# Pairs 0 and 1 of a state-space scan: block-diagonal states and split scaling, and B and C loaded four tokens to a partition

## The chip, the cores and the metric

One core of a Trainium2 chip runs the whole program. The metric is the device time of one execution in microseconds; the runs of a kernel are summed up by their median. All times and durations below are in microseconds (us) unless they are marked ns, and times "at" a point count from the start of the profiled span.

The engines are called as in the profile: PE (matrix multiply; PEld is its weight load, which overlaps), DVE (vector), ACT (scalar), POOL (GpSimd) and SP (which here only issues transfers). DMAs are issued by SP, by ACT and by POOL; those of POOL can also cast from fp32 to bf16.

## The reference

Two parts follow each other. The first is a chunked scan over 768 tokens for 4 batches of 8 heads, with head width 32 (`D`) and state width 16 (`N`):

```python
cum = np.cumsum(np.log(np.clip(a, 1e-06, 1.0))[chunk], axis=-1)
L = np.exp(cum[:, :, :, None] - cum[:, :, None, :]) * causal
M = np.einsum('bhin,bhjn->bhij', Cc, Bc) * L
y = np.einsum('bhij,bhjd->bhid', M, xc)
y += np.einsum('bhin,bhnd->bhid', Cc, state) * np.exp(cum)
state = decay_full * state + sum_j(Bc[j] * xc[j] * decay_from_j)
```

The second is a gated feed-forward network on the 3072 resulting rows of 256: `(relu(y @ w_gate) * (y @ w_val)) @ w_out`, with 1536 hidden units. Inputs and output are fp32; the kernel multiplies in bf16 where it can.

## The kernel before

**Tiles.** Tokens go in chunks of 128, two chunks make a *pair* `p` of 256 tokens of one batch. A batch has 6 chunks (`NC`), so pairs 0, 1 and 2 are batch 0 and pair 3 opens batch 1; there are 12 pairs (`NPAIR`) and 6 blocks `b` of 512 rows (`NBLK`) for the feed-forward part. The cumulative decay is one scan on DVE (`cp`, L210); small fp32 matmuls (`dec_wide`, `dec_token`, `dec_all`, L220 to L247) turn it into scale factors, which are multiplied into C, and their reciprocals into B (or, for pair 0, into x).

**One pair.** B and C are loaded as `bcr` (`load_bc`, L82). For pairs 0 to 3 (`NWIDE`) a partition holds two neighbouring tokens, so that a run of 32 fp32 values (128 B) comes in one piece; for later pairs a run is 64 B. They are scaled into bf16 `bs` (`scale_bc`, L278), transposed on PE (`transp`, L309), and copied out as `BT` (`bevac`) and as two masked versions of `CT` (`cevac`), one for each half of the heads. `G` (L374) multiplies BT and CT for four groups of heads at a time, in row tiles of 32; `gevac` (L388) copies the four banks out as `gs` with the causal mask: ACT copies two of them and POOL clears the upper triangle (`affine_select`), DVE multiplies the other two and half of one by a mask. `back` and `backevac` transpose BT back to token order (`bx`). `astep` (L413) adds B times x into the running state `A_ps` with one 128x128 by 256 matmul; `sevac` (L423) copies it out through the block mask `smask` on DVE as `Sm`, 128x256. `inter` (L484) multiplies `Sm` and CT into y, two matmuls of 128 columns for a chunk; `Dm` (L498) adds `gs` times x, 16 matmuls in column strips of 32. `yevac` (L512) copies y out as bf16 `yT`. `states` and `spread` (L438 and L456) do the states of later pairs in four column strips.

**Feed-forward.** `gvh_mm`, `gvh_relu` and `gvh_mul` do one 128-unit slice `f` of the hidden layer for one pair (256 rows), `gv` (L526) for a block of 512 rows; `fout` (L572) multiplies the hidden block by `wo`.

**Order.** Each engine runs its instructions in the order in which the program writes them (`in_order`, L15), so the order of the text is the schedule. Up to L721 it is written out by hand for pairs 0 and 1: while DVE, ACT and POOL prepare them, PE fills gaps with `keep_warm` matmuls on zeros (L200) and with slices f = 0 to 3 of pair 0. Then the loop over blocks starts (L723). In block 0, pair 1's slices 0 to 3 come first (L744), then slices 4 to 11 of the whole block; pair 2 is turned after slice 5 (L751) and turned back after slice 7, pair 3 is turned between thirds of `fout` (L783).

**Transfers.** SP issues `a`, B of pair 0, one chunk of x of pair 0, B of pair 1; ACT issues C of pair 0, the other chunk of x, C of pair 1. POOL issues the weights in pieces, cast to bf16, and chunk 0 of pair 1's x, also cast (L180). Chunk 1 of that x comes over SP (L656) and is cast by ACT (L692). B and C of pairs 2 and 3 are loaded by SP (`held`, L637, called at L657 and L693); the one-element `memset` in front of each ties its start to DVE's progress. Their scaling on POOL stands at L703 and L721. PSUM has eight banks: five shared ones and one each for the tags `y`, `tp` and `Aps`.

Of the kernel before, what the change touches and what calls it, by code (L numbers as in the profile page):

```python
# [29 lines left out]
def kernel(  # L30
# [39 lines left out]

    NWIDE = 4
    st = {}

    def place(p):
        b, c0 = p // PPB, 2 * (p % PPB)
        return b, c0, slice(c0 * 128, (c0 + 2) * 128)

# [45 lines left out]
    load_bc(0, 0, nc.sync)  # L123
# [9 lines left out]
    def cast_x(p, chunks=(0, 1)):  # L133

        b, c0, sl = place(p)
        if "x" not in st.setdefault(p, {}):
            xb = att.tile([128, 2 * NH * D], BF16, tag="xb", name="xb", bufs=6)
            st[p]["x"] = [xb[:, i * NH * D:(i + 1) * NH * D] for i in range(2)]
        for i in chunks:
# [24 lines left out]
    masks = const.tile([128, 2, 128], BF16)  # L164

    def causal(dst, n, wide):
        pattern = [[0, n], [1, 2], [2, 64]] if wide else [[0, n], [1, 128]]
        if wide:
            dst = dst.rearrange("s k (r m) -> s k r m", r=2)
# [5 lines left out]
    causal(masks[:, 1:2], 1, True)  # L175
    causal(masks[:, 0:1], 1, False)
# [3 lines left out]
    cast_x(1, (0,))  # L180
# [37 lines left out]
    wfac = glob.tile([128, NWIDE, 2, 2, 8], FP32)  # L218
# [54 lines left out]
    def cast_bc(p, eng, js):  # L273
        src, dst = views(p, js)
        for t in range(2):
            copy(eng, dst[:, :, t], src[:, :, t])

    def scale_bc(p, eng, js=slice(0, 2), f=None):  # L278
# [8 lines left out]
        for t in range(2):  # L287
            eng.tensor_tensor(  # L288
                out=dst[:, :, t], in0=src[:, :, t],
                in1=f[:, :, 4 * t:4 * t + 4].to_broadcast([128, n, 4, N]), op=ALU.mult)  # L290

# [41 lines left out]
    def cevac(p, *engs, again=None):  # L333
        s = st[p]
        s["CT"] = CT = att.tile([128, 2, 2, 128], BF16, tag="CT", name="CT")
        src = s["tp"][1].rearrange("s i m -> s (i m)")
        for t in range(2):
# [8 lines left out]
    def ct(p, i, rows=slice(0, 128), t=None):  # L346
        CT = st[p]["CT"]
# [6 lines left out]
    def split(p, ap):  # L354

        return ap.rearrange("s t (r m) -> s t r m", r=2) if p < NWIDE else ap
# [31 lines left out]
    def gevac(p, half=True, early=False, between=None):  # L388
# [3 lines left out]
        wide = p < NWIDE  # L392
        m = masks[:, int(wide):int(wide) + 1].to_broadcast([128, 4, 128])
# [10 lines left out]
        for q in (2, 3):  # L404
            nc.vector.tensor_tensor(out=d[:, q], in0=g[q], in1=m, op=ALU.mult)  # L405
        if half and not early:
# [445 lines left out]
```

## Time and profile before

| what | us |
|---|---|
| median of the 3 runs shown | 128.95 |
| lowest and highest of them | 127.25, 130.51 |
| the profiled execution | 126.84 |
| its span, first to last instruction | 124.8 |
| PE busy in the span | 120.0 |
| DVE, ACT and POOL busy | 92.7, 79.3, 43.3 |

The rows of a timeline give the start, the duration of the group, the engine, the line, the operation with what it writes and reads, the shapes and a count; the bracket says how long the engine stood idle before and what ended that. "Busy" for PE is modelled, because its matmuls overlap. The mean granted clock of PE was 0.999.

### The profile page before, as it was taken

How to read it: one execution, taken by the hardware profiler on the slowest of the kernel's cores; microseconds unless marked ns; L12 is line 12 of the kernel's file. 1: busy time of each engine (PE TensorE's matmuls, PEld its weight loads, DVE VectorE, ACT ScalarE, POOL GpSimd, SP SyncE). 2: the span in 40 equal slices, each digit the busy share in tenths (PEclk: the TensorE clock that was granted, in tenths of full speed). 3: DMA queues.
4: the chain of work that ended last, by engine and by line, in shares of the span. 5: the costliest groups of instructions: out<-in, count | busy, mean ns of one | idle time of the engine just before them, and what ended most of it. 6: DMA issues, size and time to landing. Idle time of an engine off the chain costs nothing.

```text
span 124.8 us, 3396 instructions
## 1 busy us (share of the span) xinstructions
PE 120.0 (96%) x1261; PEld 82.5 (66%) x1268; DVE 92.7 (74%) x223; ACT 79.3 (64%) x177; POOL 43.3 (35%) x80
## 2 busy tenths in 40 slices
PE   5999999999999999999999999999999999999990
PEld 2365664578885477884577875577875677864790
DVE  4678898888889955898865798855888856687510
ACT  4166777734888735787735887645987546886420
POOL 6798939531805062805021703132600033000000
PEclk9999999999999999999999999999999999999999
DMA  2999999995979999389632289912200002200022
GB/s 57 164 160 180 179 203 198 168 135 54 188 69 188 112 108 183 91 86 120 80 55 84 90 79 133 112 24 84 84 5 0 0 0 89 84 0 0 0 89 84
DMA packets 73312, 11.92 MB, mean 95 GB/s; under 512 B 66960, under 2 KB 73296, under 8 KB 73296
## 3 DMA queue, kind: packets, MB, share of 16 engines
q1 hardware_dynamic: 63408, 8.43, 44.4%
q0 software_dynamic: 6336, 2.56, 17.1%
q10 hardware_dynamic: 3552, 0.72, 3.6%
q8 instruction: 10, 0.16, 0.6%
q14 instruction: 6, 0.05, 0.1%
HBM read 11.11 MB, written 3.15 MB: 114 GB/s over the span
## 4 chain that ended last, share of the span: by engine, by line
PE 96%; DVE 1%; issue 1%
PE o L579 25%; PE gv L550 22%; PE val L534 15%; PE gate L531 13%; PE w L203 4%; PE g L382 3%; PE y L505 3%; PE tp L320 2%; PE y L494 2%; PE o L591 1%; PE d L225 1%; PE dall L243 1%; PE A_ps L450 1%; PE A_ps L419 1%; PE bt L363 1%
## 5 line engine op out<-in xcount | busy, mean ns | idle before, releaser
L579 PE MATMUL o<-wo,h 128*128 128x256 bf16 x276 | 33.1, 273 | 0.0
L538 DVE TENSOR_TENSOR h<-r,val 128x512 bf16<-128x512 bf16 x42 | 28.8, 685 | 5.5 <-ACT r L537 3.0
L537 ACT ACTIVATE r<-gate 128x512 bf16<-128x512 f32 x42 | 25.1, 597 | 8.1 <-PE gate L531 7.3
L579 PEld LDWEIGHTS <-h 128*128 128x128 bf16 x276 | 25.9, 98 | 5.4 <-issue 2.1
L560 DVE TENSOR_TENSOR h<-r,gv 128x256 bf16<-128x256 bf16 x60 | 24.8, 421 | 4.3 <-ACT r L557 3.5
L534 PE MATMUL val<-yT,wv 128*128 128x512 bf16 x84 | 25.0, 379 | 0.3
L170 POOL TENSOR_SCALAR_AFFINE_SELECT gs<-gs 128x512 bf16<-128x512 bf16 (+1 forms) x24 | 12.1, 526 | 37.3 <-ACT gs L394 37.3
L557 ACT ACTIVATE r<-gv 128x256 bf16<-128x256 f32 x60 | 22.8, 385 | 3.0 <-PE gv L550 0.8
L531 PE MATMUL gate<-yT,wg 128*128 128x512 bf16 x78 | 23.7, 379 | 0.0
L550 PE MATMUL gv<-yT,wg 128*128 128x256 bf16 x120 | 23.3, 273 | 0.0
L550 PE MATMUL gv<-yT,wv 128*128 128x256 bf16 x120 | 23.0, 273 | 0.0
L405 DVE TENSOR_TENSOR gs<-g,masks 128x512 bf16<-128x512 f32 x24 | 15.4, 684 | 5.0 <-PE g L382 4.5
L288 POOL TENSOR_TENSOR bs<-bcr,fac 128x256 bf16<-128x256 f32 x16 | 9.6, 621 | 16.1 <-DMA bcr<-in_B_dram 12.6
L534 PEld LDWEIGHTS <-wv 128*128 128x128 bf16 x84 | 8.2, 98 | 9.9
L550 PEld LDWEIGHTS <-wv 128*128 128x128 bf16 x120 | 11.7, 98 | 1.9 <-DMA wv<-in_moe_w_val_dram 0.3
L550 PEld LDWEIGHTS <-wg 128*128 128x128 bf16 x120 | 11.2, 98 | 1.9 <-issue 0.2
L394 ACT CAST gs<-g 128x512 bf16<-128x512 f32 x12 | 7.1, 590 | 8.4 <-PE g L382 8.4
L262 ACT CAST yT<-y 128x512 bf16<-128x512 f32 (+1 forms) x14 | 7.1, 527 | 7.7 <-PE y L505 4.1
L531 PEld LDWEIGHTS <-wg 128*128 128x128 bf16 x84 | 7.8, 98 | 6.3
L461 DVE TENSOR_TENSOR Sm<-A_ps,smask 128x256 bf16<-128x256 f32 x15 | 5.8, 418 | 6.3 <-PE A_ps L450 6.3
L608 ACT COPY ob<-o 128x512 f32<-128x512 f32 x10 | 5.9, 585 | 4.7 <-PE o L579 4.7
L344 DVE TENSOR_SCALAR CT<-tp,tmask 128x256 bf16<-128x256 bf16 x23 | 7.0, 343 | 0.3 <-PE tp L629 0.3
(92 smaller groups left out, 106.5 us busy)
## 6 DMA issues: line engine op xcount, KB each, us to landing
xr<-in_x_dram SPq DMA_DIRECT2D x20, 128.0 KB, 3.4
out_dram<-ob SPq DMA_DIRECT2D x10, 256.0 KB, 2.2
bcr<-in_C_dram SPq DMA_DIRECT2D x16, 64.0 KB, 3.1
bcr<-in_B_dram SPq DMA_DIRECT2D x16, 64.0 KB, 3.1
wg<-in_moe_w_gate_dram POOLq DMA_DIRECT2D x3, 256.0 KB, 5.0
wv<-in_moe_w_val_dram POOLq DMA_DIRECT2D x3, 256.0 KB, 6.0
wo<-in_moe_w_out_dram POOLq DMA_DIRECT2D x3, 256.0 KB, 5.2
bcr<-in_B_dram SPq DMA_DIRECT2D x4, 128.0 KB, 6.6
```

The source lines that it names most:

```text
L170: nc.gpsimd.affine_select(out=dst, in_=dst, pattern=pattern, compare_op=ALU.is_ge, fill=0.0, base=0, channel_multiplier=-1)
L262: (eng.copy if eng is nc.scalar else eng.tensor_copy)(out=out, in_=in_)
L288: eng.tensor_tensor(out=dst[:, :, t], in0=src[:, :, t], in1=f[:, :, 4 * t:4 * t + 4].to_broadcast([128, n, 4, N]), op=ALU.mult)
L405: nc.vector.tensor_tensor(out=d[:, q], in0=g[q], in1=m, op=ALU.mult)
L531: nc.tensor.matmul(out=g, lhsT=wg[:, k, fs], rhs=yT[:, k, tk], start=(k == 0), stop=(k == 1))
L534: nc.tensor.matmul(out=v, lhsT=wv[:, k, fs], rhs=yT[:, k, tk], start=(k == 0), stop=(k == 1))
L537: nc.scalar.activation(r, g, AF.Relu)
L538: nc.vector.tensor_tensor(out=fst[b][:, f], in0=r, in1=v, op=ALU.mult)
L550: nc.tensor.matmul(out=gv_[:, j], lhsT=(wg, wv)[j][:, k, fs], rhs=yT[:, k, tk], start=(k == 0 and not (early and j)), stop=(k == 1), skip_ ...
L557: nc.scalar.activation(r[:, 0:256], fst[b, f, u][:, 0], AF.Relu)
L560: nc.vector.tensor_tensor(out=fst[b][:, f, u * 256:(u + 1) * 256], in0=fst.pop((b, f, u, "r"))[:, 0:256], in1=fst.pop((b, f, u))[:, 1], op ...
L579: nc.tensor.matmul(out=o[:, ts % 2], lhsT=fst[b][:, f, ts * 128:(ts + 1) * 128], rhs=wo[:, f], start=(f == 0 and new), stop=(f == NF - 1), ...
```

## The change

It has two halves. *States*: `astep` uses four column strips of 32 and writes only the 64 columns that hold the diagonal blocks; for the states read by pairs 0 and 1 `sevac` is an ACT copy of 128x64, and `inter` multiplies the four 32x32 blocks on their own diagonal tiles of the array (8 matmuls a chunk in place of 2). Later states are spread on DVE as before. Pair 1's B is scaled half on DVE and half on POOL. *Loads*: B of pair 0 comes with four tokens to a partition on 64 partitions, and ACT casts it in two copies; B of pairs 2 and 3 share one tile, 64 partitions each with four tokens to a partition, and so do their C (`load_quad`). They are scaled together on POOL, turned together after slice 8 and turned back together between thirds of `fout`. A run of B or C is then 256 B, and a load has half as many pieces.

Some steps move with it. Both chunks of pair 1's x come over SP, issued behind the first mask product of pair 0, and are cast by POOL and ACT; POOL's cast load of one chunk is gone. Slice 3 of pair 0 and a part of `dec_all` change places around `Dm(1)`. The last two pieces of `wo` are issued ahead of the scaling of pairs 2 and 3, the cast load of pair 2's x behind it. One of four later `keep_warm` matmuls of 512 columns is left out. `cevac` writes its two versions of pair 1 ahead of and behind DVE's share of `yevac(0)`.

The diff, cut to its core (a third mask for four tokens, `R(p)` for the number of tokens to a partition, and the reading of the shared tiles in `ct` are left out):

```diff
+def load_quad(j):
+    if not quad:
+        quad["bcr"] = raw.tile([128, NH, 2, 4, N], FP32, tag="quad", name="bcr4", bufs=1)
+    bcr = quad["bcr"]
+    nc.vector.memset(bcr[:, 0, j, 0, 0:1], 0.0)
+    for p in (2, 3):
+        b, c0, sl = place(p)
+        ps = slice(64 * (p - 2), 64 * (p - 1))
+        nc.sync.dma_start(
+            out=bcr[ps, :, j].rearrange("p h r n -> p h (r n)"),
+            in_=(B, C)[j][b, :, sl, :].rearrange("h (p r) n -> p h (r n)", r=4))
...
-load_bc(0, 0, nc.sync)
+b0r = glob.tile([64, NH, 4, N], FP32)
+nc.sync.dma_start(
+    out=b0r.rearrange("p h r n -> p h (r n)"),
+    in_=B[0, :, 0:256, :].rearrange("h (p r) n -> p h (r n)", r=4))
...
-cast_x(1, (0,))
...
+def dec_quad(dst, p):
+    b, c0, _ = place(p)
+    w, o = c0 // HC, (c0 % HC) * 128
+    ps = slice(64 * (p - 2), 64 * (p - 1))
+    for r in range(4):
+        nc.tensor.matmul(
+            out=dst[ps, r], lhsT=cp[:, o + r:o + 256:4],
+            rhs=pick[:, w, 8 * b:8 * b + 8], start=(r == 0), stop=True,
+            tile_position=(0, 64 * (p - 2)), skip_group_check=True)
...
+def scale_quad(eng):
+    quad["bs"] = bs = att.tile([128, 2, 4, 128], BF16, tag="bs4", name="bs4", bufs=1)
+    for j in (1, 0):
+        for t in range(2):
+            hs = slice(4 * t, 4 * t + 4)
+            eng.tensor_tensor(
+                out=bs[:, j].rearrange("s r (q t n) -> s r t q n", q=4, t=2)[:, :, t],
+                in0=quad["bcr"][:, hs, j].rearrange("s q r n -> s r q n"),
+                in1=qfac[:, j, :, hs].to_broadcast([128, 4, 4, N]), op=ALU.mult)
+def turn_quad():
+    quad["tp"] = tp = mm.tile([128, 2, 4, 128], BF16, tag="tp", name="tp4")
+    for j in range(2):
+        for r in range(4):
+            nc.tensor.transpose(out=tp[:, j, r], in_=quad["bs"][:, j, r], identity=ident)
+    quad["BT"] = att.tile([128, 4, 128], BF16, tag="BT4", name="BT4", bufs=1)
+    quad["CT"] = att.tile([128, 2, 4, 128], BF16, tag="CT4", name="CT4", bufs=1)
+    for p in (2, 3):
+        st.setdefault(p, {})["BT"] = quad["BT"][:, 2 * (p - 2):2 * (p - 1)]
+def bevac_quad(eng):
+    copy(eng, quad["BT"].rearrange("s k (m r) -> s k r m", r=4),
+         quad["tp"][:, 0].rearrange("s r (k m) -> s k r m", k=4))
+def cevac_quad(eng, t):
+    dst = quad["CT"][:, t].rearrange("s r m -> s (r m)")
+    src = quad["tp"][:, 1].rearrange("s r m -> s (r m)")
+    if eng is nc.scalar:
+        eng.mul(dst, src, tmask[:, t:t + 1])
+    else:
+        eng.tensor_scalar_mul(dst, src, tmask[:, t:t + 1])
+def back_quad(eng):
+    bt = mm.tile([128, 4, 128], BF16, tag="tp", name="bt4")
+    for k in range(4):
+        nc.tensor.transpose(out=bt[:, k], in_=quad["BT"][:, k], identity=ident)
+    bx = att.tile([128, 4, 128], BF16, tag="bx4", name="bx4", bufs=1)
+    copy(eng, bx.rearrange("s k m -> s (k m)"), bt.rearrange("s k m -> s (k m)"))
+    for p in (2, 3):
+        st[p]["B"] = [bx[:, 2 * (p - 2) + i] for i in range(2)]
...
+def cevac(p, *engs, again=None, ts=(0, 1)):
...
-def gevac(p, half=True, early=False, between=None):
...
+        if q in after:
+            after[q]()
...
-    nc.tensor.matmul(
-        out=A_ps[0], lhsT=st[p]["B"][i], rhs=st[p]["x"][i],
-        start=(c == 0), stop=(c == NC - 2), skip_group_check=True)
+    xi = st[p]["x"][i].rearrange("s (t q d) -> s q t d", t=2, q=4)
+    for q in range(4):
+        nc.tensor.matmul(
+            out=A_ps[0][32 * q:32 * q + 32, 0, 0:64].rearrange("p (t d) -> p t d", t=2),
+            lhsT=st[p]["B"][i][:, 32 * q:32 * q + 32], rhs=xi[:, q],
+            start=(c == 0), stop=True, tile_position=(0, 32 * q),
+            skip_group_check=True)
...
 def sevac(p, i):
-    if 2 * (p % PPB) + i == NC - 1:
+    c = 2 * p + i + 1
+    if c == NC:
         return
-    S[2 * p + i + 1] = n = att.tile([128, 2, 128], BF16, tag="Sm", name="Sm", bufs=5)
-    nc.vector.tensor_tensor(out=n, in0=A_ps[0], in1=smask, op=ALU.mult)
+    if c < 2 * NTILE:
+        S[c] = n = att.tile([128, 64], BF16, tag="Sd", name="Sd")
+        nc.scalar.copy(out=n, in_=A_ps[0][:, 0, 0:64])
+    else:
+        S[c] = spread_one(0)
...
+def spread_one(k):
+    n = att.tile([128, 2, 128], BF16, tag="Sm", name="Sm", bufs=5)
+    a = A_ps[0][:, 0, 64 * k:64 * k + 64].rearrange("p (t o d) -> p t o d", t=2, o=1)
+    nc.vector.tensor_tensor(
+        out=n.rearrange("p t (q d) -> p t q d", q=4),
+        in0=a.to_broadcast([128, 2, 4, D]),
+        in1=smask.rearrange("p t (q d) -> p t q d", q=4), op=ALU.mult)
+    return n
...
+        if p < NTILE:
+            new = opening(s, t)
+            for q in range(4):
+                r = slice(32 * q, 32 * q + 32)
+                nc.tensor.matmul(
+                    out=s["y"][t][r, i].rearrange("s (r m) -> s r m", r=2),
+                    lhsT=Sm[r, 32 * t:32 * t + 32], rhs=ct(p, i, r, t=t),
+                    start=new, stop=True, tile_position=(32 * q, 32 * q),
+                    skip_group_check=True)
+            continue
...
 new_bs(0)
 dw = bank("dw", (128, 2, 8))
 dec_wide(dw, 0, True)
+b0s = glob.tile([64, 4, 128], BF16)
+for t in range(2):
+    nc.scalar.copy(
+        out=b0s.rearrange("s r (q t n) -> s r t q n", q=4, t=2)[:, :, t],
+        in_=b0r.rearrange("s (t q) r n -> s r t q n", t=2)[:, :, t])
+tpb = bank("tpb", (128, 4, 64), BF16)
+for r in range(4):
+    nc.tensor.transpose(out=tpb[:, r], in_=b0s[:, r], identity=ident[0:64, 0:64])
+st[0]["BT"] = att.tile([128, 2, 128], BF16, tag="BT", name="BT")
+copy(nc.scalar, st[0]["BT"].rearrange("s k (m r) -> s k r m", r=4),
+     tpb.rearrange("s r (k m) -> s k r m", k=2))
 d01 = mm.tile([128, 2, 2, 8], FP32, tag="Aps", name="d01")
 dec_token(d01[:, 0], 0, True)
-cast_bc(0, nc.scalar, B_)
 scale_bc(0, nc.vector, C_, dw)
 r0 = const.tile([128, 2, 8], FP32)
 nc.vector.reciprocal(r0, d01[:, 0])
 to_x(0, nc.gpsimd, r0.rearrange("s i h -> s (i h)"))
-transp(0, 0, True)
-bevac(0, nc.scalar)
 transp(0, 1, True)
...
-gevac(0, between=lambda: backevac(0, nc.scalar))
-new_x(1)
-nc.vector.memset(st[1]["xr"][0:1, 1, 0, 0:1], 0.0)
-load_x(1, 1, nc.sync)
-held(2, with_x=False)
-keep_warm(3)
-d23 = mm.tile([128, 2, 2, 8], FP32, tag="tp", name="d23")
-dec_wide(d23[:, 0], 2, True)
+def load_x1():
+    new_x(1)
+    nc.vector.memset(st[1]["xr"][0:1, :, 0, 0:1], 0.0)
+    for i in range(2):
+        load_x(1, i, nc.sync)
+gevac(0, between=lambda: backevac(0, nc.scalar), after={2: load_x1})
+load_quad(1)
+keep_warm(2)
+d23 = mm.tile([128, 4, 8], FP32, tag="tp", name="d23")
+dec_quad(d23, 2)
 astep(0, 0)
-dec_wide(d23[:, 1], 3, False)
-nc.scalar.copy(out=wfac[:, 2:4, 1], in_=d23)
+sevac(0, 0)
+dec_quad(d23, 3)
+nc.scalar.copy(out=qfac[:, 1], in_=d23)
 keep_warm(1)
-sevac(0, 0)
 scale_bc(1, nc.vector, C_)
-scale_bc(1, nc.gpsimd, B_)
+scale_bc(1, nc.vector, B_, ts=(1,))
+scale_bc(1, nc.gpsimd, B_, ts=(0,))
 weights(4, 8)
+new_xb(1)
+def x1(eng, i):
+    copy(eng, st[1]["x"][i], st[1]["xr"][:, i].rearrange("s h d -> s (h d)"))
+x1(nc.gpsimd, 0)
 Dm(0, True)
 inter(0, 1)
+transp(1, 1, True)
 astep(0, 1)
-transp(1, 1, True)
 transp(1, 0, True)
+cevac(1, nc.vector, ts=(0,))
 yevac(0, nc.scalar, nc.vector)
 bevac(1, nc.scalar)
-cevac(1, nc.vector)
+cevac(1, nc.vector, nc.vector, ts=(1,))
 sevac(0, 1)
...
 back(1)
 gevac(1, early=True, between=lambda: backevac(1, nc.scalar))
-copy(nc.scalar, st[1]["x"][1], st[1]["xr"][:, 1].rearrange("s h d -> s (h d)"))
-held(3, with_x=False)
+x1(nc.scalar, 1)
+load_quad(0)
 weights(8, NF)
 weights_out(0, 4)
-for f in (1, 2, 3):
+for f in (1, 2):
     gvh_mm(0, f, 0)
     gvh_relu(0, f, 0)
+dall = mm.tile([128, HC, 2, NB, 8], FP32, tag="tp", name="dall")
+dec_all(dall, range(2))
 astep(1, 0)
 sevac(1, 0)
-nc.vector.reciprocal(wfac[:, 2:4, 0], wfac[:, 2:4, 1])
-new_bs(2)
-scale_bc(2, nc.gpsimd)
+nc.vector.reciprocal(qfac[:, 0], qfac[:, 1])
 weights_out(4, 8)
 weights_out(8, NF)
+scale_quad(nc.gpsimd)
+cast_x(2)
 Dm(1, "shared")
 inter(1, 0)
 inter(1, 1)
 astep(1, 1)
 yevac(1, nc.scalar, nc.vector)
-dall = mm.tile([128, HC, 2, NB, 8], FP32, tag="tp", name="dall")
-dec_all(dall, range(HC))
+gvh_mm(0, 3, 0)
+gvh_relu(0, 3, 0)
+dec_all(dall, range(2, HC))
 for f in range(4):
     gvh_mul(0, f, 0)
 for w in range(2):
     nc.scalar.copy(
         out=fac[:, :, w * HC:(w + 1) * HC, 1, :].rearrange("p b k h -> p k b h"),
         in_=dall[:, :, w])
-new_bs(3)
-cast_x(2)
-scale_bc(3, nc.gpsimd)
...
         if b == 0:
-            if f == 5:
-                turn(P)
-                tevac(P, nc.scalar, nc.vector)
-            if f == 7:
-                back(P)
-                backevac(P, nc.vector)
+            if f == 8:
+                turn_quad()
...
+            if f == 10:
+                cevac_quad(nc.scalar, 1)
...
             if third == 1:
-                turn(Q)
-                tevac(Q, nc.scalar, nc.vector)
+                back_quad(nc.scalar)
...
-        back(Q)
-        backevac(Q, nc.vector)
```

## The prediction

> **What bounds the kernel now.** I read the page first (shares, then the 40 slices), then the chain of waits over the opening, then the timeline of each engine from 5 to 16 us, then the DMA issues one at a time.
>
> ```profile
> PE 120.0 (96%) x1261; PEld 82.5 (66%) x1268; DVE 92.7 (74%) x223; ACT 79.3 (64%) x177; POOL 43.3 (35%) x80
> ...
> PEclk9999999999999999999999999999999999999999
> DMA  2999999995979999389632289912200002200022
> ```
>
> PE's 96% is two different things. From 15.5 us on the chain is PE behind PE, a 512-column pair each 0.43 us, and nothing else ends last. Before that PE is busy on paper (4.02 us are warming matmuls) while the end is set by a relay between engines. So a gain or loss is either an earlier or later start of the dense stretch, or PE work or PE waits inside it. The relay:
>
> ```profile
> 5.34 0.50 ACT L262 CAST bs<-bcr 128x128 bf16<-128x128 f32 x2 [3.04 <-DMA bcr<-in_B_dram]
> ...
> 6.22 0.29 PE L320 MATMUL tp<-ident,bs 128*128 128x128 bf16 x2
> ...
> 7.16 0.40 PE L382 MATMUL g<-CT,BT 32*128 32x256 bf16 x8
> ...
> 7.67 1.05 POOL L299 TENSOR_TENSOR xb<-xr,r 128x512 bf16<-128x512 f32 x1 [0.29 <-DMA xr<-in_x_dram]
> ...
> 7.68 1.29 DVE L405 TENSOR_TENSOR gs<-g,masks 128x512 bf16<-128x512 f32 x2 [0.20 <-PE g L382]
> ...
> 8.68 1.03 POOL L170 TENSOR_SCALAR_AFFINE_SELECT gs<-gs 128x512 bf16<-128x512 bf16 x2
> ...
> 9.76 0.41 PE L505 MATMUL y<-gs,xb 128*32 128x128 bf16 x16
> ...
> 10.78 0.59 DVE L344 TENSOR_SCALAR CT<-tp,tmask 128x256 bf16<-128x256 bf16 x2
> ...
> 11.50 0.40 PE L382 MATMUL g<-CT,BT 32*128 32x256 bf16 x8
> ...
> 13.75 0.41 PE L505 MATMUL y<-gs,xb 128*32 128x128 bf16 x16
> ```
>
> Pair 0's B lands at 5.34; G(0) runs at 7.16; from 7.68 to 11.37 DVE hardly rests; POOL, late because x of pair 0 lands only at 7.6, releases Dm(0) at 9.76; DVE's C copies release G(1) at 11.50. In the dense stretch one other arrival is near the edge:
>
> ```profile
> 17.76 1.19 POOL L288 TENSOR_TENSOR bs<-bcr,wfac 128x256 bf16<-128x256 f32 x2 [1.99 <-DMA bcr<-in_B_dram]
> ...
> 22.43 1.19 POOL L288 TENSOR_TENSOR bs<-bcr,wfac 128x256 bf16<-128x256 f32 x2 [0.22 <-DMA bcr<-in_B_dram]
> ```
>
> These are B of pairs 2 and 3, issued at 10.39 and 14.04: 7.2 and 8.2 us on the way, because the weights share the DMA engines (205 GB/s from 13.7 to 21.5 us, of which SP's own 393 KB are about 50).
>
> What a packet costs, from three stretches with one kind of load (64 B runs, 128 B runs, 1 KB output rows; the last columns are clock, DMA share and GB/s):
>
> ```profile
> 41.00:43.00 2.00, 2.00 (x14) 0.98 (x12) 1.85 (x5) 1.62 (x4) 0.00 (x0) 1.00 0.93 95
> ...
> 43.00:44.50 1.50, 1.50 (x14) 1.05 (x13) 1.17 (x3) 0.79 (x2) 0.64 (x2) 1.00 1.02 152
> ...
> 49.00:49.50 0.50, 0.50 (x12) 0.38 (x5) 0.50 (x2) 0.50 (x2) 0.00 (x0) 1.00 1.11 343
> ```
>
> 95, 152 and 343 GB/s over 16 engines are 10.8, 13.5 and 48 ns a packet; a line through them puts 256 B at about 18 to 19 ns.
>
> **The change, part by part.**
>
> *B of pair 0 as 512 packets of 256 B.* Behind `a` the SP queue shares each DMA engine with ACT's queue: 64 packets of 13.5 ns beside 64 others is 1.7 us, which with `a` through at 2.9 (153 GB/s flow from 2 to 3 us) and 0.7 us to its signal (seen at 3.6) gives the 5.34 seen. 32 of 19 beside 32 of 13.5 are 1.0 us: B lands near 4.65. Ends: 5.34 (bytes alone count), 4.65; I take 4.7. ACT then casts two 64x256 blocks, 0.43 each by the 128x256 cast of x (0.50 for both before, now about 0.8): done by 5.5. Four transposes (0.22 issued) replace two (0.11), but PE is held until 5.54 by dw in any case; `dec_token` now stands behind them (0.32) and ends at 6.1, before C's scaled block (6.16). So the C transposes stay at 6.22, G(0) at 7.16: 0. Without the early landing: casts to 6.15, transposes and `dec_token` to 6.7, G(0) 0.5 late. x of pair 0, behind B on SP and no longer joined by the POOL cast of pair 1, comes at 7.0 to 7.5.
>
> *POOL and DVE to G(1).* POOL loses a DMA issue (0.90) and half of pair 1's B scaling (0.42); with x at 7.2 its selects end near 9.3 instead of 9.71. DVE loses the 0.41 spread at 9.23 but gains memsets (0.06 each) and B's half (0.35 by the neighbouring 128x128 row), and its yT copy now stands behind the first C copy (0.34). Sum: 9.24 + 0.06 + 0.69 + 0.35 + 0.34 + 0.45 + 0.34 less overlaps of 0.1: C done near 11.3 (11.37 before). Dm(0) comes 0.3 earlier, G(1) 0.1 earlier: DVE takes the rest of the gain back. wv (landed at 11.06) is awaited inside this as before.
>
> *x of pair 1 on SP.* Two loads issued at 8.4 (behind the first mask) replace one at 9.35 and one POOL cast. The old one landed at 12.85: less 1.3 us until data flows (as for `a`, 0.80 to 2.1) and 0.7 to the signal, 1.5 of transfer. Two from 9.75 are then done at 9.75 + 3.0 + 0.7 = 13.4, or at 12.2 by the 152 GB/s of an empty queue. ACT wants it at 13.0. Between: 0.15 late, and behind it on ACT stand two relus, the new state copy and y. I charge +0.15.
>
> *States as diagonal blocks.* Three 0.41 spreads leave DVE, three 128x64 copies come to ACT at about 0.21 (the 128x32 copy took 0.18, the 128x96 one 0.24). The last spread, 13.86 to 14.28, had held inter(1,1); the copy ends near 14.1: -0.15. Each state step is four 64-column matmuls on four column strips (12 such issue in 0.10 to 0.18) for one of 0.11: -0.05 each, all but one in the opening's slack. inter has 8 small matmuls for 2; no row has its shape. Ends: 0.11, four at once as for the 16 of L505, or 0.44, one after another. I take 0.11, since its blocks share neither rows nor strips.
>
> The weight loader stands 0.21 us idle before each row-tiled G and before the 128-wide load behind it, but at 52.46 a 128-wide matmul follows column strips with no gap. So three new changes (one around inter(1,.), two around state(2,0), which stood between `fout` matmuls) cost 0 to 0.6; I take a third, +0.2. The Trainium skill (TensorEngine Tiling (Array Packing), Key Properties) says that every change of the tiling mode drains TensorE; by that rule all three cost 0.21 and the sum below would be 0.4 higher.
>
> *f = 3, dall.* Before, six dall matmuls (0.81) behind y(1) and DVE's first product (15.42) both held gvh(0,0,1) to 15.47. Now 0.44 of f = 3 and 0.27 of dall stand there, and 0.54 of dall stands ahead of Dm(1), where PE waits for masks. DVE's product decides: y 0.1 earlier, so -0.1. `keep_warm` (3 to 2) takes 0.21 from a stretch where PE waits for POOL: 0.
>
> *Quads.* 12 transposes before, 12 after. ACT's copies grow (0.58 and 0.69 at f = 8 and 10 for 0.37 at f = 5; it has 0.27 spare per 0.87 us step), DVE's shrink (0.61 for 0.60 and 0.60). Covered by PSUM banks and PE's own 0.45 of transposes; `bx4` (ACT, near 27.9) is just in time for the state step at 28.0: 0 to +0.2, taken as 0. POOL's four 0.60 scalings are the same four, but all must end before the turn at 21.5 (17.2 + five steps of 0.87): B of both pairs must land by 20.3, where pair 3's had until about 25. SP's queue: x to about 12.5, then 262 KB of C and 262 KB of B. At 128 B, SP got 50 GB/s, 41 ns a packet and engine: 13.5 its own, 27.5 waiting. 256 B: 46.5 ns if only its own part grows, 88 GB/s, B at 19.2; if all grows like its own part (1.42 times), 71 GB/s, B at 20.6; with no gain 50 GB/s, B at 23.7. I take 19.2, since the packet was mostly waiting: no wait.
>
> Sum: -0.1 (G(1)), +0.15 (x), -0.15 (state copy), -0.1 (f = 3), +0.2 (mode changes): 0.0. The profiled run took 126.84 us, its span 124.8 and 2.0 around it; the median of the runs shown is 128.95 (127.25 to 130.51). Forecast: no change, 126.8 on the profiled run's scale, 129.0 on the median's.
>
> **Rivals.**
> 1. *PE waits at the turn for B of pairs 2 and 3* (the other side). For: one deadline for two pairs, two more POOL weight loads pulled ahead of it, today's 8.2 us. Against: half the packets. Price: landing + 1.25 (two scalings) - 21.5; 0.35 at 71 GB/s, 3.4 at 50, so 129.3 to 132.4. It decides from a landing after 20.3, and passes 2% after 22.9.
> 2. *B of pair 0 doesn't land earlier.* G(0) 0.5 late, DVE passes all of it on: 129.5.
> 3. *Diagonal blocks run one by one.* inter(0,1) hides behind DVE, the two of pair 1 do not: +0.66, less 0.1 of slack: 129.6. No row speaks for it. The Trainium skill (TensorEngine Tiling (Array Packing), Gotcha 1: PSUM Pressure) says that different row tiles can't use one PSUM bank at the same time, and all four blocks write one bank; no run here shows it so far.
> 4. *Landings bring more.* x of pair 0 at 6.9 and pair 1's at 12.2, C scaled in 0.5 as at 5.68: -0.15, -0.2, -0.3: 128.3.
>
> **How the numbers follow.** Forecast 0.46 (128.5 to 129.5), rival 1 0.25, rival 2 0.08, rival 3 0.07, rival 4 0.14. About 2% (2.6 us) is what a measurement of this kernel can tell from no change. Only rival 1's far half passes it: 0.12, and 0.06 for the scatter of runs on top of rivals 1 to 3: slower 0.18. No case gains 2.6; rival 4 with the scatter (1.3% to either side of the median) gives faster 0.08; same 0.74. The range takes in rival 4 and the runs' scatter below (127.6) and rival 1 to a landing at 22.4 us above (131.2).
>
> **What would show it.** B's cast at 4.7 and G(0) at 7.2; Dm(0) near 9.4, G(1) near 11.4; inter's 8 matmuls issued in 0.11 to 0.15; gvh(0,0,1) at 15.3 to 15.6; transposes of the quad straight behind the val matmuls of f = 8, the scaling on POOL ended before. Wrong if PE stands before the turn, if G(0) slips, or if the dense stretch starts after 16.

## The result, and the profile after

The changed kernel takes 133.98 us (median of 4 runs, 133.29 to 134.19) against 129.73 for the kernel before on the same chip (4 runs, 127.25 to 130.65): 1.045 times, 95% interval 1.0313 to 1.0586. The forecast was 129.0. The runs of the kernel before lie near 127 or near 130.5, with a few between; ratios here leave the longer, disturbed runs out, medians take in all. The profiled execution of the changed kernel took 133.29, its span 131.4 (before 126.84 and 124.8).

The posts of the relay that the prediction read, as starts in us from each span's beginning:

| | before | forecast | after |
|---|---|---|---|
| cast of B of pair 0 (ACT) | 5.34 | 4.7 | 6.14 |
| G(0) | 7.16 | 7.2 | 8.80 |
| Dm(0) | 9.76 | 9.4 | 13.47 |
| G(1) | 11.50 | 11.4 | 16.05 |
| Dm(1) | 13.75 | none given | 18.87 |
| gvh(0,0,1), the dense stretch begins | 15.47 | 15.3 to 15.6 | 20.63 |
| end of the span | 124.8 | 124.8 | 131.4 |

Of 6.6 us, 5.2 are lost before the dense stretch and 1.4 in it (109.3 to 110.8). The timeline of the changed kernel's opening (start, duration, engine, line, operation, and in brackets the idle time before it with its releaser):

```profile
6.14 0.71 ACT L722 CAST b0s<-b0r 64x256 bf16<-64x256 f32 x2 [3.84 <-DMA b0r<-in_B_dram]
...
6.90 0.29 PE L727 MATMUL tpb<-ident,b0s 64*128 64x64 bf16 x4 [1.52 <-ACT b0s L722]
...
7.23 0.73 ACT L295 COPY BT<-tpb 128x256 bf16<-128x256 bf16 x1 [0.38 <-PE tpb L727]
...
8.60 0.17 ACT L743 COPY wfac<-d 128x16 f32<-128x16 f32 x1 [0.29 <-PE d L258]
...
8.80 0.61 PE L457 MATMUL g<-CT,BT 32*128 32x256 bf16 x8
...
10.52 1.03 PEld L248 LDWEIGHTS d<-pick,cp 64*64 64x64 f32 x8 [0.84 <-issue]
...
13.47 0.62 PE L608 MATMUL y<-gs,xb 128*32 128x128 bf16 x16
...
14.02 0.40 PE L588 MATMUL y<-CT,Sd 32*32 32x128 bf16 x8
```

B arrives 0.8 later, not 0.6 sooner. PE takes its instructions in order, so it stands 1.52 us in front of the transposes of `b0s`, with `dec_token` and C's transposes queued behind. G(0) is 1.64 late: 0.80 from the arrival, 0.21 from a longer cast, some 0.3 on ACT from a copy of BT that takes 0.73 for 0.37, and some 0.3 in which ACT then waits for the decay matmuls queued behind `b0s` (row 8.60, whose result G(0) needs). The eight decay loads of one pair, 1.03 at 10.52, had taken a third of that in the kernel before:

```profile
8.35 0.33 PEld L225 LDWEIGHTS d<-pick,cp 64*64 64x64 f32 x8 [0.42 <-issue]
```

From G(0) to G(1) the rows of PE that kept their shape are a third to a half longer than before (G(0) 0.61 for 0.40, Dm(0) 0.62 for 0.41, two transposes 0.39 for 0.28). The clock says why. First the page's slices, then four stretches of the same trace (length; busy us and instructions of PE, PEld, DVE, ACT, POOL; granted clock; DMA share; GB/s):

```profile
PEclk9965579999999999999999999999999999999998
```

```profile
6.00:7.00 1.00, 0.10 (x4) 0.10 (x4) 0.00 (x0) 0.71 (x2) 0.36 (x1) 1.00 1.62 129
...
7.50:8.00 0.50, 0.50 (x8) 0.30 (x7) 0.26 (x1) 0.50 (x2) 0.01 (x1) 0.55 1.53 170
8.00:12.00 4.00, 4.00 (x37) 2.45 (x37) 3.05 (x10) 1.75 (x6) 2.93 (x5) 0.50 0.90 145
...
18.00:20.00 2.00, 2.00 (x50) 1.40 (x49) 0.91 (x4) 1.30 (x5) 2.00 (x5) 1.00 0.18 8
```

PE was busy 0.10 of the microsecond from 6 to 7; at 7.6 its granted clock is halved, stays at 0.50 for ten microseconds and is back at 1.00 at 17.8. In the dense stretch the turn of the quad and G(2):

```profile
25.62 1.19 POOL L325 TENSOR_TENSOR bs<-bcr,qfac 128x256 bf16<-128x256 f32 x2 [2.38 <-DMA bcr<-in_B_dram]
...
26.27 0.59 PE L637 MATMUL val<-yT,wv 128*128 128x512 bf16 x2
...
26.86 0.45 PEld L334 LDWEIGHTS <-bs 128*128 128x128 bf16 x8 [0.49 <-POOL bs L325]
26.87 0.62 PE L334 MATMUL tp<-ident,bs 128*128 128x128 bf16 x8
...
27.52 1.30 ACT L295 COPY BT<-tp 128x512 bf16<-128x512 bf16 x1 [0.45 <-PE tp L334]
...
30.98 0.28 PE L457 MATMUL g<-CT,BT 32*128 32x256 bf16 x3
...
31.57 0.37 PE L457 MATMUL g<-CT,BT 32*128 32x256 bf16 x5 [0.30 <-DVE bcr L752]
```

B of pairs 2 and 3 comes last. The 0.49 is idle time of the weight loader; PE itself loses about 0.17, since a pair of 512 columns takes 0.43 from start to start and the turn starts 0.60 behind the last `val`. The copy of BT takes 1.30 us where 0.58 was forecast; G(2) is then split by a wait (its eight matmuls start at 30.98 and 31.57).

### The profile page after: what moved, and what is told of

The parts are those of the page before. It is cut to its first block, busy times and chain, and to the rows that moved or that the text cites. A ratio compares the mean times of both kernels' runs of the same rounds, so it can differ in the third digit from the quotient of the medians.

```text
span 131.4 us, 3466 instructions
## 1 busy us (share of the span) xinstructions
PE 124.7 (95%) x1302; PEld 85.0 (65%) x1302; DVE 90.8 (69%) x216; ACT 82.9 (63%) x181; POOL 42.8 (33%) x80
## 4 chain that ended last, share of the span: by engine, by line
PE 73%; ACT 1%; issue 0%; DVE 0%
PE o L682 23%; PE gv L653 17%; PE val L637 11%; PE gate L634 11%; PE y L608 3%; PE g L457 3%; PE y L597 1%; PE tp L389 1%; PE o L694 1%; ACT yT L295 1%; PE A_ps L548 1%; DVE ob L697 0%; PE bt L355 0%; PE A_ps L500 0%
## 5 line engine op out<-in xcount | busy, mean ns | idle before, releaser
L634 PE MATMUL gate<-yT,wg 128*128 128x512 bf16 x84 | 25.0, 379 | 0.0
L653 PE MATMUL gv<-yT,wg 128*128 128x256 bf16 x120 | 23.9, 278 | 0.3 <-ACT yT L295 0.3
L653 PE MATMUL gv<-yT,wv 128*128 128x256 bf16 x120 | 23.6, 277 | 0.0
L295 ACT CAST yT<-y 128x512 bf16<-128x512 f32 (+1 forms) x14 | 8.2, 624 | 8.2 <-PE y L608 4.1
L653 PEld LDWEIGHTS <-wg 128*128 128x128 bf16 x120 | 11.4, 100 | 2.0 <-issue 0.2
L525 DVE TENSOR_TENSOR Sm<-A_ps,smask 128x256 bf16<-128x256 f32 x17 | 6.6, 419 | 7.1 <-PE A_ps L548 6.5
L415 DVE TENSOR_SCALAR CT<-tp,tmask 128x256 bf16<-128x256 bf16 x19 | 5.9, 344 | 2.9 <-PE tp L389 2.7
```

Source lines behind the costliest of these rows:

```text
L295: (eng.copy if eng is nc.scalar else eng.tensor_copy)(out=out, in_=in_)
L634: nc.tensor.matmul(out=g, lhsT=wg[:, k, fs], rhs=yT[:, k, tk], start=(k == 0), stop=(k == 1))
L653: nc.tensor.matmul(out=gv_[:, j], lhsT=(wg, wv)[j][:, k, fs], rhs=yT[:, k, tk], start=(k == 0 and not (early and j)), stop=(k == 1), skip_ ...
```

## The experiments

Five suspects stood at the start: the *lateness* of B of pair 0; the *clock*, lost in the stall before `tpb`; the *steps* in the quads' decay loads and copies; the *states* half (blocks one by one, the split scaling); and the *turn*, where PE waits for the quads' B (the prediction's rival 1). Where an expectation numbers its theories, the numbers hold for that run. "B of pair 0 as before" below means its load, cast, transposes and copy in the old form.

**1. The changed kernel with B of pair 0 as before.**

```diff
-b0r = glob.tile([64, NH, 4, N], FP32)
...
+load_bc(0, 0, nc.sync)
...
+cast_bc(0, nc.scalar, B_)
...
+transp(0, 0, True)
+bevac(0, nc.scalar)
```

> The changed kernel with B of pair 0 loaded, cast and turned as before (128 partitions, 128 B runs). Theory 1 (the late B of pair 0 lets PE stand for 1.5 us, the granted clock halves from 7.6 to 17.7 us and stretches the opening): B's cast back near 5.3, granted clock 1.0 throughout, Dm(0) near 10 to 10.8 in place of 13.5, time 129 to 131. Rival theory 2 (the cost is the work for pairs 2 and 3: strided loads of the decay factors on PE, slow copies on ACT, B late at the turn): still over 132.

132.42 (4 runs, 131.81 to 132.63), 1.0412 of before (1.0377 to 1.0448). By the expectation's figures that is theory 2: B of pair 0 is only a part of it, since 132.42 is above even the longest run of the kernel before on this chip (130.72). Its profile shows a second thing: the matmuls run at half rate from the first on, until about 17 (two transposes 0.40 for 0.28), though the granted clock is recorded as 0.997. So this run doesn't part the price of the quads from that of such an opening.

**2. The kernel before with only B of pair 0 in its new form** (the reverse of the edit above).

> The kernel before with only B of pair 0 in the new form. Theory 1: B's cast near 6.1, PE stands from 5.3 to 6.9, the clock halves in the opening, 3 us slower or more (131.5 to 134). Theory 2: within 1 us of before.

131.25 (129.84 to 131.76), 1.031 (1.023 to 1.0391). PE stands 1.43 before `tpb`, G(0) comes at 8.77, the granted clock is at half from 7.9 to 18.2, Dm(0) comes at 12.99. One load in another form, with its cast, transposes and copy, costs 4 us.

**3. The changed kernel with seven filler matmuls in the stall.**

```diff
+keep_warm(7)
 tpb = bank("tpb", (128, 4, 64), BF16)
```

> The changed kernel with seven more matmuls of 512 columns on zeros where PE waits for B of pair 0 (5.3 to 6.9 us). Theory 1, by the clock: granted clock stays 1.0, G(0) stays late (near 8.3), time 130 to 131.5. If the late landing alone costs and not the clock: no change, 133 to 134. Theory 2: no change either.

134.51 (132.84 to 136.05), 1.0462 (1.0437 to 1.0487): nothing gained by the median, nor by the ratio, which rests on the two runs of 132.84 and 133.06 (granted clock 0.987); the other two took 135.96 and 136.05 (0.949). In the profile, of the run of 135.96, the fillers do hold the clock to 11.8 us; then it is lost all the same, until 25.5, behind the stretch of the decay matmuls, whose loads take 1.03 us for eight at full clock too:

```profile
9.64 1.03 PEld L248 LDWEIGHTS d<-pick,cp 64*64 64x64 f32 x8 [0.42 <-issue]
10.83 1.03 PEld L248 LDWEIGHTS d<-pick,cp 64*64 64x64 f32 x8
```

So the stall isn't the only thing that costs the clock: the steps cost by themselves, and the clock goes while they are paid.

**4. The kernel before with only the states half** (`astep`, `sevac`, `spread`, `inter`, `cevac` and pair 1's scaling of the change).

> The kernel before with only the diagonal states and pair 1's split scaling. By the prediction's terms (state copy -0.15, mode changes +0.2, split scaling near 0): within 0.5 us of before, granted clock 1.0. If the diagonal blocks or the moved work on ACT cost the most (theory 3): 131 or more.

129.35 (127.28 to 130.47), 1.006 (0.9984 to 1.0136): no difference that can be told. By this run the states fall out as a main cause, and so does rival 3: 16 blocks of 32x32 take 0.45 in the trace of the changed kernel (19.20), where four 128x128 matmuls took 0.54 before.

**5. B of pair 0 as before, and the decay weights laid out once without a step.**

```diff
+cpq = glob.tile([2 * BH, 4, H // 4], FP32)
+nc.vector.tensor_copy(cpq, cp.rearrange("p (m r) -> p r m", r=4))
...
-        out=dst[ps, r], lhsT=cp[:, o + r:o + 256:4],
+        out=dst[ps, r], lhsT=cpq[:, r, o // 4:o // 4 + 64],
```

> The changed kernel with B of pair 0 as before, and with the decay products copied once on DVE so that the decay matmuls of pairs 2 and 3 load 64 neighbouring columns in place of every fourth. Theory 2a (those strided weight loads, 1.03 us for 8 in place of 0.33, stand in PE's queue between G(0) and Dm(0), add 1.4 us and are too little work to keep the clock open): Dm(0) near 10 where the clock is 1.0, time 128 to 129.5, 3 us less than with B of pair 0 alone undone. Rival 2b (late B of pairs 2 and 3 or ACT's slow copies): 131.5 or more, as without this edit.

130.99 (129.92 to 132.51), 1.0213 (1.0173 to 1.0253), against 1.0412 with the step. The two figures stand for different openings. The runs of 132.51 and 132.06 are no shorter than those of experiment 1, and the profile of the first is at half rate from the start too: its eight loads take 0.93 for 1.03, and Dm(0) comes at 12.29 for 12.49. Only the two runs of 129.92, with a recorded clock of 1.0, are faster than any of experiment 1. So in an opening at half rate the edit is worth some 0.2; that it keeps an open clock open is argued from two runs without a profile.

**6. The changed kernel with that edit and the seven fillers.**

> The changed kernel with B of pair 0 in its new form, the same copy for the decay matmuls, and seven matmuls on zeros where PE waits for that B. If theory 1 (late B of pair 0 costs by the clock) and 2a both hold: granted clock 1.0 in most runs, G(0) near 8.4, time 129 to 130.5. If late B costs by itself: 131 or more.

132.84 (131.11 to 133.96), 1.045 (1.0411 to 1.0489). Its profiled run is the fastest of the six (131.11) and the only one with a recorded clock of 1.0 (the others 0.984 to 0.997). It holds the clock throughout, Dm(0) at 11.50 for 13.47, and gives much of that back: PE's row at the turn now shows a wait of 1.07, where that of the changed kernel shows none. Repairing the opening uncovers the turn.

**7. A probe:** the kernel before with additions whose results nothing uses: loads of B of another batch in the three shapes, decay matmuls with weights at a step of 1, 2 and 4, and four ACT copies of 512 elements.

> The kernel before with probes whose results nobody reads, in the last two blocks where no load is under way: three loads of 128 KB (128 partitions in 128 B runs; 64 partitions in 256 B runs; twice 64 partitions in 256 B runs of half the heads), twelve fp32 weight loads of 64 columns (four each at a step of 1, 2 and 4 elements), and four ACT copies of 128x512 bf16 from PSUM (plain; writing every second element; writing every fourth; writing in order and reading in steps). By the prediction: 256 B runs land sooner than 128 B runs (0.6 against 0.9 us of transfer), weight loads all alike, copies all 0.58. By the profile of the changed kernel: the 64-partition load no sooner, step 4 about three times as long as step 1 or 2, the copy that writes every fourth element 1.3, the one that writes in order 0.6.

128 KB land after 3.1 us with 128 B runs on 128 partitions (the DMA engines busy 0.57 of the time) and after 3.0 with 256 B runs on 64 (busy 0.19); as two halves, each 2.5. These are single landings, but the wider runs gain next to nothing even with the emptier engines. Weight loads: 129 to 138 ns at steps 1 and 2, 213 at step 4. The copies, plain, writing every second and every fourth element, and writing in order with stepped reads:

```profile
120.20 0.58 ACT L783 COPY probe_f<-probe_e 128x512 bf16<-128x512 bf16 x1 [2.17 <-PE probe_e L780]
120.68 0.74 ACT L784 COPY probe_f<-probe_e 128x512 bf16<-128x512 bf16 x1
121.26 1.31 ACT L786 COPY probe_f<-probe_e 128x512 bf16<-128x512 bf16 x1
122.29 0.71 ACT L788 COPY probe_f<-probe_e 128x512 bf16<-128x512 bf16 x1
```

The same permutation costs 1.31 if the step is on the writing side and 0.71 if it is on the reading side.

**8. Experiment 2 with the seven fillers.**

> The kernel before with only B of pair 0 in the new form, and seven matmuls on zeros where PE waits for it. Without them this form alone cost 3.1% and the clock fell at 7 us. Theory 1, by the clock: clock 1.0, G(0) near 8.5, time 128.5 to 129.5. If lateness alone costs: 131 as without.

128.94 (128.34 to 129.12), 1.0128 (1.009 to 1.0165) against 1.031 without: of B of pair 0's price more than half is the clock. In its profile the nine fillers had not opened the clock (`dw` 0.61 for 0.42); the seven do, and though they push G(0) back to 9.36, Dm(0) comes at 11.91 for 12.99.

**9 to 12. A ladder at an open clock:** 14 fillers at the start for nine, on the kernel before; with the states; with the quads too; and with the quads mended.

```diff
-keep_warm(9)
+keep_warm(14)
```

Mended means the edit of 5, the loads of pairs 2 and 3 taking turns between the column halves, one filler given back, and BT written in order:

```diff
-    copy(eng, quad["BT"].rearrange("s k (m r) -> s k r m", r=4),
-         quad["tp"][:, 0].rearrange("s r (k m) -> s k r m", k=4))
+    copy(eng, quad["BT"].rearrange("s k (m r) -> s k m r", r=4),
+         quad["tp"][:, 0].rearrange("s r (k m) -> s k m r", k=4))
...
-        for r in range(4):
+        for r in range(4):
+            for p in (2, 3):
```

> The kernel before, with 14 filler matmuls of 128x512 at the start in place of 9. In the profile of before the nine take 4.02 us (0.45 each, 1.26 to 5.28) and the work after them runs at full speed; in the profile of the kernel with only the states changed the same nine take 4.02 and all that follows is at half rate until 16.9, for a span 3.9 us longer (128.7 against 124.8). Theory 1 (the opening's rate is decided by whether the fillers last until the clock opens): every run is near 127 to 129, none near 130.5, the fillers end between 5.8 and 7.3 and everything behind them is at full rate, 0.28 for two transposes. Theory 2 (what comes after the fillers, not they, decides): the time is that of before plus the length added, 1.1 to 2.1 us in all runs, and half-rate openings stay as frequent: 128 to 133 us.

128.08 (10 runs, 127.43 to 128.83), where the kernel before spread over 126.79 to 130.81 in 13 runs on the same chip: none is left near 130.5, and the profiled one is at full rate behind its fillers. Theory 1. None of the runs of the kernel before near 130.5 has a profile, but experiment 7, which is the same kernel up to 92 us, shows such an opening: Dm(0) at 12.11 for 9.76, at half rate from the first on.

> The kernel before with only the states changed (diagonal blocks, pair 1's scaling split), and 14 fillers in place of 9. If the states half is neutral, as both theories have it, this is the kernel before with 14 fillers to within 0.7 us; if the blocks or the split cost something that the chances of the opening have hidden so far, it is 1 us or more above.

129.25 (128.08 to 130.38): 1.2 above, by the expectation's figures the answer that the states cost something. In its profile, of the slowest run, the fillers last 6.13 us for 4.81, and PE waits 0.36 for `Sd` (ACT), 0.32 and 0.75 for casts of x. The last two aren't in the states' code, and experiment 15, which has no states, shows one of them too (0.42). What the diagonal states cost, from nothing to 1.2, stays open.

> The changed kernel with B of pair 0 as before, and 14 fillers in place of 9: against the one with only the states and 14 fillers, this is the price of the four-tokens-a-partition layout of pairs 2 and 3. Theory 1 (the layout has a price of its own: 16 decay loads in one column half at a step of four, 2.1 us instead of 0.7, then 0.5 at the turn, 0.4 at G(2) and 0.3 behind Dm(3)): 2.2 to 3.5 us above it, Dm(0) 1.2 to 1.8 us later against the end of the fillers. Theory 2 (its price was the clock alone, lost while the slow loads ran): within 1 us, since the clock is open from the start.

132.34 (131.86 to 135.14), 3.1 above the states alone, in theory 1's range. But the clock that was open at the start did not stay open: in the profile it is at half from 11.3 to 14.7, behind the slow loads. So the 3.1 are the layout's own price and that loss of the clock together, and theory 2 is not refuted by this run; the next one takes the slow loads away.

> The same as the kernel with states, quads and 14 fillers, with three parts of the layout's price taken away: the decay weights are laid out once by a copy on DVE so that they load without a step, the loads of pairs 2 and 3 alternate between the two column halves, BT's copy writes in order and reads with a step, and the third filler behind G(0) is back. Theory 1: the 16 loads take 0.7 to 0.8 us instead of 2.1, BT's copy 0.7 instead of 1.3, G(2) isn't split; 1.5 to 2.5 us faster than the one not mended, and 0.3 to 1.2 above the one with only the states, what is left being the wait at the turn and the late copy of yT. Theory 2 (the price lies in the dense stretch's other waits): at most 0.7 us faster.

130.43 (129.97 to 132.37), 1.9 less, and the granted clock stays at 1.00 through the opening. The 16 loads take 0.55 instead of 2.06, Dm(0) comes 4.3 us behind `dw` instead of 5.7, BT's copy takes 0.58. The largest wait that is left is in one row: the sooner the opening ends, the longer PE stands at the turn.

```profile
9.05 0.55 PEld L249 LDWEIGHTS d<-pick,cpq 64*64 64x64 f32 x16 [0.42 <-issue]
```

```profile
22.69 1.19 POOL L331 TENSOR_TENSOR bs<-bcr,qfac 128x256 bf16<-128x256 f32 x2 [3.55 <-DMA bcr<-in_B_dram]
```

```profile
23.94 0.62 PE L340 MATMUL tp<-ident,bs 128*128 128x128 bf16 x8 [1.18 <-POOL bs L331]
```

**13. The mended kernel with the turn two steps later (and ACT's copy of CT one step later) and yT written in order.**

```diff
-                if f == 8:
+                if f == 10:
                     turn_quad()
...
-                 dst[:, t].rearrange("q (i m r) -> q i r m", i=2, r=R(p)),
-                 s["y"][t].rearrange("q i (r m) -> q i r m", r=R(p)))
+                 dst[:, t].rearrange("q (i m r) -> q i m r", i=2, r=R(p)),
+                 s["y"][t].rearrange("q i (r m) -> q i m r", r=R(p)))
```

> The mended kernel (14 fillers, B of pair 0 as before, decay loads without a step, BT in order), with yT's copies written in order too and the turn of the quad two steps later, at f = 10. In the mended kernel PE stood 1.18 us at the turn for B, whose scaling on POOL began at 22.7. Theory 1 (that wait and the copy of yT are what is left of the layout's price): the wait is gone, the gv behind Dm(3) no longer waits 0.30 for yT, 1.0 to 1.6 us below the mended kernel's 130.4. Theory 2 (the time comes back at G(2), which needs the same B, or in the state step behind it): at most 0.5 us below.

128.87 (127.49 to 129.71), 1.0115 of before (1.0001 to 1.0228), on another chip than the ladder, where the mended kernel stood at 1.0217 (1.013 to 1.0305): some 1.3 us less by the ratios, whose intervals overlap, 1.6 by the medians. The profiles are clearer: PE no longer stands at the turn, yT's copies take 0.38 for 0.78 us, and the dense stretch is 109.3 us long (17.25 to 126.6), what it was before the change, where the mended kernel's is 111.6. The turn and yT's copy were what was left of it; the two edits were made together and not parted.

**14. The mended kernel with 512 KB of `wo` asked for behind the quad's scaling** (`weights_out(4, 8)` and `(8, NF)` moved below `scale_quad`; yT in order).

> The mended kernel with yT's copies in order, and the second and third part of wo (512 KB of 1.3 MB that POOL asks for between 14.2 and 17.9) asked for behind the scaling of the quad's B. Theory 1 (B of the quads lands late because these weights share the engines of the DMA with it): it lands 1 us or more sooner than 6.6 us after its issue, the wait at the turn falls from 1.18 to under 0.4, and the time is 0.8 to 1.4 us below the mended kernel's 130.4. Theory 2 (B waits behind C in SP's own queue, packet by packet, whatever POOL asks for): the landing stays at 6.3 to 6.9 us and the wait at 1.0 or more; the time falls by at most the 0.3 of yT, or rises if wo comes late for the out-projection.

133.06 (131.96 to 134.0). B was issued at 14.39 and its scaling began at 22.90, as in the mended kernel (14.29 and 22.69): with 512 KB less beside it, it comes no sooner. PE waits 1.69 at the turn, then 1.5 for casts of x and 0.62 for `wo`. So these 512 KB don't set B's arrival. The rest of what POOL asks for was left as it was; B's place in SP's queue behind x and C is another candidate, and neither was varied.

**15. The kernel before with 14 fillers, B of pair 0 in its new form, its BT written in order.**

> The kernel before with B of pair 0 in the new form, 14 fillers at the start, and BT of pair 0 copied in order of writing. The fillers end near 6.0 where the clock opens early, b0s is ready near 6.85, so PE still stands up to 0.9 us. Theory 1 (the new load lands no sooner, and beside the clock it costs its lateness alone): 0.7 to 1.3 us above the kernel before with 14 fillers (128.1), G(0) at 8.4 to 8.7 for 7.95 there, BT's copy 0.4 instead of 0.73. Theory 2 (with clock and copy made even it costs nothing): within 0.3 us of it.

128.15 (127.84 to 128.52), 1.0103 (1.0071 to 1.0135), where the kernel with 14 fillers alone had 1.0057 (1.0013 to 1.0101) on another chip: 0.6 us by the ratios and 0.1 by the medians, between the two theories. G(0) is 0.24 later; the fillers here run to 6.3, so that PE hardly stands for B.

**16. The whole change with every repair.**

> The whole change, B of pair 0 in its new form too, with every repair: 14 fillers at the start, decay loads without a step and in alternating halves, BT of pair 0, BT of the quad and yT copied in order of writing, and the turn of the quad at f = 10. If the causes found are all of them, it is within 1 us of the kernel before with 14 fillers (127.4 to 128.8 in its ten runs), against 133.98 for the change as it stands: 127.8 to 129.5, no row of the clock under 0.9, G(0) 0.2 to 0.4 later than without the new B. If B of pair 0 and the quads' loads, which only here share a queue again, get into each other's way, 130 or more.

129.25 (128.75 to 129.66), 1.0122 (1.004 to 1.0203), against 1.045 for the change as it stands. B cast at 5.74, G(0) 8.05, Dm(0) 10.40, G(1) 12.33, dense stretch from 16.30. So the causes found are most of it. Of the 1.2% left, 14 fillers by themselves are about half (experiment 9); in the profile PE also waits 0.9 for a cast of x of pair 2.

**17. Experiment 13 with nine fillers.**

> The kernel with the quad's turn late, states changed and B of pair 0 as before, with the nine fillers of the kernel before. By the clock theory its runs spread as those of the kernel before do, from about 126.8 to 130.8, by whether the nine fillers open the clock; its best is 126.5 to 127.3, 1 us under what 14 fillers gave. If the layout keeps a price of its own, its best is above 128.

127.88 in one run, 130.63 to 130.8 in three; the profiled one of the three is an opening at half rate (Dm(0) at 11.83). The best is 0.8 above the best of before on the same chip (127.08), so by this single run the layout may still cost some tenths. No version here was faster than the kernel before.

## Why the prediction was wrong, step by step

- *B of pair 0 at 4.7.* Failed, the first step. The line "a packet costs 10.8, 13.5, 48 ns" was drawn through rates, and then used as if halving the packets halved the wait. Cast times of the old form are 5.34 to 5.65 in 12 profiles (middle 5.42), of the new form 5.68 to 6.16 in 7 (middle 5.82): 0.4 later. The probe shows nearly equal landings for equal bytes.
- *"Without the early landing ... G(0) 0.5 late"* (rival 2). The branch was right and its price wrong: G(0) was 1.64 late, and rival 2 had PE's stall in it but not what the stall does to the clock. Of experiment 2's 3.1%, the fillers of experiment 8 gave 1.8 back.
- *`dec_quad`.* No term of the sum. The text costs the transposes and the copies of the quads and takes the decay matmuls for what they were. They load weights at a step of four, all of one pair into one column half: 1.03 for eight against 0.33, on the path to Dm(0).
- *"`keep_warm` (3 to 2) ... 0".* By itself it was never isolated. What the fillers stand for, the granted clock, has no term in the sum at all. It is the largest part of what B of pair 0 cost (2.3 of 4 us, experiments 2 and 8); its share in the whole change was not measured by itself.
- *ACT's copies 0.58 and 0.69.* The first took 1.30 (written at a step of four), and pair 0's 0.73. Row and column counts were read, the step wasn't.
- *Quads: B at 19.2, no wait.* Failed as a landing (POOL began its scaling at 25.62), but in the changed kernel it cost only some 0.17 at the turn, since the dense stretch began 5.2 late. Rival 1 (0.25) shows where the opening is repaired, in place and in mechanism. By its formula, landing + 1.25 - 21.5, mended kernel 12 gives: B at 22.6, less the 1.05 by which its dense stretch begins later, 21.55, so 1.3; measured 1.18. That landing lies between "all grows like its own part" (20.6) and "no gain" (23.7).
- *States, x of pair 1, mode changes, f = 3.* Sum forecast 0; experiment 4 measured 1.006 (0.9984 to 1.0136). Right within what that run can tell; experiment 10 leaves up to 1.2 open, and the single terms weren't tested.
- *Rival 3.* Refuted: 16 blocks in 0.45, where one after another would be 0.88 by the prediction's 0.44 for eight. The Trainium skill's rule cited with it (TensorEngine Tiling (Array Packing), Gotcha 1: PSUM Pressure) doesn't hold for these blocks in one bank; the measurement decides.

In sum: 5.2 us of opening are 1.64 to G(0), 2.07 from G(0) to Dm(0) (slow loads and half rate) and 1.45 from there to the dense stretch at half rate. The 1.4 in the dense stretch, by the starts of the same rows in both traces, are 0.3 up to the first `fout` (0.17 of it the turn), 0.6 in the `fout` of block 0 (0.4 where G(2) is split) and 0.5 behind it (0.3 where PE waits for yT's copy).

## What to carry to other kernels

Before moving a load's consumer, list what stands behind it in the in-order queue and ask what the engine's clock does while it stands: here one late load cost 4 us, of which fillers in its stall gave 2.3 back. Cost every operand by its step and not only by its shape, and put the step of a permuting copy on the side that reads. A relay that gets quicker meets arrivals that were hidden, so a deadline must be checked for the fast case, not the slow one.

## What the runs showed of the hardware

- TensorE's clock. The fillers show where it opens: 14 of them took 4.72 to 6.13 us in the profiles that have them; nine took 3.52 in the changed kernel, and 4.02 both in the kernel before, which is at full rate behind them, and in experiment 1, which isn't. In the changed kernel it falls back behind a stall of 1.5 us (0.4 busy of the 2.1 us before 6.9), and comes back at 17.8, 1.0 into a run of gate and value matmuls (from 16.8). How long it stays at half goes in steps: 3.41 us in experiment 11, 10.24 in the changed kernel and in experiment 2, 13.65 in experiment 3, which are one, three, three and four times 3.41. The Trainium skill (TensorE: Matmul & The Clock Gate, Part 1: The HAM clock gate) tells of a free-running activity window of about 3.4 us, so that the number of slow matmuls varies from run to run; the spread of the fillers and these steps agree. The Trainium skill's advice on the same page to avoid idle gaps over about 3 us (Why this matters for your kernels) is too mild for this trace, where 1.5 us were enough. The length of the stall alone doesn't decide: in experiment 14 PE stood 1.69 us at the turn, in the middle of dense work, and the granted clock stayed at 1.00; in experiment 11 it fell with PE busy 3.26 of the 3.41 us before, most of them with the slow loads and short matmuls.
- In openings where the clock did not open (the profiles of experiments 1, 4, 5, 7 and 17), it is recorded as 0.997 to 1.0 while matmuls run at half rate (two transposes 0.40 for 0.28). There the slices can't be trusted before the first change of the clock; durations can.
- Eight loads of 64x64 fp32 weights take 0.33 us when they alternate between column halves, 0.54 in one half, 1.03 in one half at a step of four. In the probe a step of two costs nothing. The Trainium skill (SBUF — State Buffer, Specifications (TRN2)) says that a 16-byte line needs two hits to run at full rate; for the loads that agrees (step 2 is two fp32 to a line, step 4 one). ACT's writes don't: every fourth bf16 element is two to a line, and takes 1.31 for 0.58.
